# Layer 2's second token block: a step's seven w_ch1 products in one run, then its w_ch2 products in one run

## The chip, the cores and the metric

The kernel runs on one core of one Trainium2 chip. The metric is the device time of one execution in microseconds (us); lower is better. The median of three runs before the change is 657.65 us (657.61 to 657.93), so a difference of 0.2%, about 1.3 us, is near what a measurement of this kernel can tell from none.

## The reference

Three layers follow one another on 4 x 576 tokens of 512 features, all in float32: a retention (linear attention with decay), a gated layer that mixes along the sequence, and a plain feed-forward layer. The change lies in the third, which the kernel calls layer 2:

```python
def _moe2_ref(x, g_ln, w_ch1, w_ch2) -> np.ndarray:
    mu = np.mean(x, axis=-1, keepdims=True)
    var = np.mean((x - mu) ** 2, axis=-1, keepdims=True)
    xn = (x - mu) / np.sqrt(var + 1e-06) * g_ln
    ch = np.maximum(xn @ w_ch1, 0.0) @ w_ch2
    return (x + ch).astype(np.float32)
```

w_ch1 is 512 x 2048 and w_ch2 is 2048 x 512.

## The kernel before

**Three matmuls for one product.** Each float32 operand is split into a high part, rounded to the format that TensorE takes, and a low part, the rest. `mm3` (lines 134 to 137) forms high x high, high x low and low x high into one PSUM bank. So all products of the kernel come in threes.

**Layer 2.** Its 18 tiles of 128 tokens are worked in three blocks of six tiles. A block has eight steps (`NQ = 8`), so s runs from 0 to 23; a step makes 256 of the 2048 hidden features, as two halves of 128. Both dimensions of a step's first multiplication are halved and its eight block products are replaced by seven (Strassen's scheme in Winograd's form): features and weights are first added and subtracted (`mix_features`, `mix_w1`), then seven products are made, w0 to w6, of six matmuls of 384 columns each, and their results are added up by VectorE (DVE) into four quarters of hidden features. ScalarE (ACT) takes the relu of a quarter as its high part h (line 1175), and DVE subtracts it from the value for the low part (line 1176). `product` issues one of the seven, `hidden` a step's seven in four parts: w0 and w5, w1 and w2, w3 and w4, w6.

**The second multiplication** is `project(s, q)` for the four quarters q: three token tiles, each by `mm3` with 512 columns, nine matmuls, added over the eight steps of a block in six PSUM banks (`o_t`). Two banks are left for the seven products. In blocks 0 and 1 the parts of step s alternate with the four `project(s - 1, q)`. The third block (s of 16 and more, `hidden_kept`) only makes and keeps hidden features, seven products in one run; its second multiplication is done at the end by a seven-product scheme of its own (`multiply_kept`), whose weights `turning` prepares during blocks 1 and 2.

**Order.** Nothing is scheduled by a tool: each engine runs its instructions in the order in which the code emits them, and waits in place for semaphores. The loop `for s in range(NB * NQ)` is that order. Within a step, for q = 0 to 3, it emits a part of `hidden`, one `project`, one piece of `turning` (GpSimd, called POOL, and ACT), the split of w_ch2 rows into high and low (`split_w2`: ACT line 944, POOL line 945), their loading (`load_w2`) and saving for the third block (`save_w2`), then `ahead`, which loads rows, normalises them for the next block (DVE, ACT, POOL), writes the turned rows to DRAM (`norm`, line 994), loads them back as features and splits these (`mix_features`, `split_features`), and last `fetch_w1`, which brings the split w_ch1 of a later step back from DRAM. All transfers are issued by one queue, SP, in that order, and an SP instruction that waits holds back all behind it.

**Buffers.** w_ch1 has two (`w1_at`, steps even and odd), w_ch2 one for each half (`w2_at`), rows seven, taken in turn (`row_tile`).

Of the kernel before, what the change touches and what calls it, by code (L numbers as in the profile page):

```python
# [31 lines left out]
TB = 6  # L32
# [69 lines left out]
def kernel(  # L102
# [844 lines left out]
    def save_w2(s):  # L947
        if NF <= s < 2 * NK:
            p, i = divmod(s - NF, 2)
# [31 lines left out]

    def norm(p, n):
        z = yh[n]

        def stats():
# [4 lines left out]
            def rest():  # L990
                normed(z, st)
                yield
                t = row_tile()
                dve.transpose(out=t, in_=z)
                nc.sync.dma_start(out=z_dram[n], in_=t)
# [36 lines left out]
    def split_features(blk):  # L1032
        b11, b21, b12, b22 = halves(blk)
        for i, y in ((0, b11), (4, mixed(0)), (5, mixed(1)), (6, mixed(2)), (2, mixed(3)), (1, b21), (3, b22)):
# [138 lines left out]
    def relu(s, i, v):  # L1173
        t = h_t[s, i] = h_at[i][s % len(h_at[i])]
        act.activation(out=t[:, 0], in_=v, func=ACTF.Relu)  # L1175
        dve.scalar_tensor_tensor(  # L1176
# [3 lines left out]
    def hidden(s):  # L1180
# [5 lines left out]
        for part in ((0, 5), (1, 2), (3, 4), (6,)) if s else ((5, 0, 2, 4), (1,), (3,), (6,)):  # L1186
            for w in part:
# [9 lines left out]
                elif w == 2 or w == 4:  # L1197
                    dve.tensor_tensor(out=t, in0=v, in1=u if w == 2 else t, op=ALU.add)
                    if w == 4:
                        relu(s, 3, t)  # L1200
                else:
# [4 lines left out]
                    relu(s, {1: 0, 3: 2, 6: 1}[w], v)  # L1206
                if last:
                    free(bk[a])
            yield

# [48 lines left out]
    def project(s, q):  # L1259
# [4 lines left out]
        if p == 0 and q == 0:  # L1264
            o_t[blk] = [bank() for j in range(TB)]
        first, last = p == 0 and i == 0, p == NQ - 1 and i == 1
        w = w2_at[i]
        for j in reversed(range(TB // 2)):
# [3 lines left out]
            if last:  # L1272
                n = blk * TB + h * TB // 2 + j

                o = row_tile()
                dve.tensor_tensor(
                    out=turned_row(o), in0=ps.rearrange("p (f k c) -> p f k c", k=KE, c=32),
                    in1=o_s.pop(n).rearrange("p (f k c) -> p f k c", k=KE, c=32), op=ALU.add,
                )
                free(ps)  # L1280
                store_row(n, o)
# [112 lines left out]
    def ahead(blk, q):  # L1394
# [4 lines left out]
        if q == 1 and blk:  # L1399
            for j in reversed(range(TB // 2, TB)):  # L1400
                load_rest((blk - 1) * TB + j)
        if blk + 1 < NB:
# [6 lines left out]
            if q in (13, 20):  # L1409
                load_features(blk + 1, q // 20)  # L1410
            if q in (15 + blk, 22 + blk):
# [12 lines left out]
            if q >= 24 and q != 28:  # L1424
# [3 lines left out]
        if q == 4 * NQ - 1:  # L1428
            for j in reversed(range(TB // 2)) if blk + 1 < NB else range(TB):
                load_rest(blk * TB + j)  # L1430
            if blk + 1 == NB:
                o_s[None] = row_tile()
# [140 lines left out]
```

## Time and profile before

| | us |
|---|---|
| median of three runs | 657.65 |
| the profiled execution | 658.18 |
| its span, first to last instruction | 656.2 |
| around the span | 1.98 |
| TensorE (PE) busy, share of the span | 646.8, 99% |
| VectorE (DVE) busy | 455.0, 69% |
| GpSimd (POOL) busy | 321.6, 49% |
| ScalarE (ACT) busy | 316.0, 48% |

Two records stand for a matmul: PE is the multiplication, PEld the loading of its stationary operand. A busy PE is not a PE at its best: matmuls overlap, so each lasts longer in the records than the time to the next one's start. The distance from start to start is what a run of matmuls costs. In the trace, layer 2's first step begins at 282.0 us, block 1 (s = 8) at 399.26, the third block's first step without `project` (s = 17) at 540.73, and `multiply_kept` at 591.7.

### The profile page before, as it was taken

Reading aid. Unit: us, or ns where it says so; the run is one execution under the profiler, and the core shown is the slowest. Engines: PE = TensorE matmul, PEld = TensorE weight load, DVE = VectorE, ACT = ScalarE, POOL = GpSimd, SP = SyncE. Lnnn points to the kernel's source line nnn. Section 1 sums busy time; section 2 is a strip of 40 time slices with the busy share of each in tenths; the row PEclk is TensorE's granted clock in tenths of the full one; section 3 lists DMA queues with packets and bytes.
Section 4 is the critical chain, followed back from the end, with each engine's and each line's share of the span. In section 5 each row is a group of like instructions: output and inputs, shape, how many; then the busy total and the mean of one; then the engine's idle time right before and its main releaser. Section 6 shows DMA issues by size and latency. Waiting matters only on the chain.

```text
span 656.2 us, 12551 instructions
## 1 busy us (share of the span) xinstructions
PE 646.8 (99%) x4422; PEld 591.2 (90%) x4422; DVE 455.0 (69%) x906; ACT 316.0 (48%) x656; POOL 321.6 (49%) x315
## 2 busy tenths in 40 slices
PE   8998999999999999999999999999999999999997
PEld 5998899899889889899888999888988899999996
DVE  4698779789989885868888533555533345458894
ACT  4556795365286466434453533233535313335443
POOL 2467868225326528945655793265559743310000
PEclk9999999999999999999999999999999999999999
DMA  8999447777797695489896867799999699999634
GB/s 306 383 368 371 166 111 213 252 238 233 259 298 232 189 242 145 151 312 384 319 309 238 274 205 261 247 366 387 347 332 360 216 295 350 371 379 405 243 129 161
DMA packets 99264, 181.22 MB, mean 276 GB/s; under 512 B 9857, under 2 KB 46849, under 8 KB 97410
## 3 DMA queue, kind: packets, MB, share of 16 engines
q1 hardware_dynamic: 99202, 180.42, 81.5%
q8 instruction: 35, 0.57, 0.3%
q14 instruction: 27, 0.22, 0.1%
HBM read 122.97 MB, written 56.62 MB: 274 GB/s over the span
## 4 chain that ended last, share of the span: by engine, by line
PE 71%; DVE 3%; ACT 3%; DMA 1%; issue 1%; POOL 1%; SPq 0%; POOLq 0%; ACTq 0%; DVEq 0%
PE b L137 20%; PE b L136 20%; PE b L135 20%; PE b L864 4%; PE b L1341 3%; PE b L1342 2%; DVE c L163 1%; DMA raw<-in_w_ch_dram 1%; ACT t L695 1%; PE b L798 1%; POOL vnl L721 1%; PE b L797 0%; ACT t L692 0%; ACT raw L160 0%; DVE bs L669 0%
## 5 line engine op out<-in xcount | busy, mean ns | idle before, releaser
L137 PE MATMUL b<-fe,w 128*128 128x384 f32 x336 | 113.1, 337 | 0.0
L135 PE MATMUL b<-fe,w 128*128 128x384 f32 x336 | 112.9, 336 | 0.0
L136 PE MATMUL b<-fe,w 128*128 128x384 f32 x336 | 112.7, 335 | 0.0
L137 PE MATMUL b<-w,h 128*128 128x512 f32 (+1 forms) x270 | 98.1, 363 | 0.0
L136 PE MATMUL b<-w,h 128*128 128x512 f32 (+1 forms) x270 | 98.0, 363 | 0.0
L135 PE MATMUL b<-w,h 128*128 128x512 f32 (+1 forms) x270 | 96.8, 358 | 0.0
L945 POOL TENSOR_TENSOR w<-raw_w,w 128x512 fp32r<-128x512 f32 x30 | 39.6, 1320 | 59.0 <-ACT w L944 53.3
L135 PEld LDWEIGHTS b<-fe,w 128*128 128x128 f32 x336 | 63.1, 188 | 3.0
L136 PEld LDWEIGHTS b<-fe,w 128*128 128x128 f32 x336 | 63.1, 188 | 2.8
L137 PEld LDWEIGHTS b<-fe,w 128*128 128x128 f32 x336 | 63.0, 188 | 0.0
L137 PEld LDWEIGHTS b<-w,h 128*128 128x128 f32 x270 | 51.0, 189 | 7.6
L160 ACT ACTIVATE raw<-raw 128x512 f32<-128x512 f32 x44 | 29.9, 679 | 56.2 <-DVE b L158 49.3
L136 PEld LDWEIGHTS b<-w,h 128*128 128x128 f32 x270 | 50.9, 189 | 6.3 <-POOL w L945 0.2
L135 PEld LDWEIGHTS b<-w,h 128*128 128x128 f32 x270 | 51.0, 189 | 6.0 <-issue 0.2
L1175 ACT ACTIVATE h<-b 128x384 fp32r<-128x384 f32 x32 | 15.7, 492 | 83.8 <-DVE b L1204 54.1
L665 POOL TENSOR_TENSOR st<-st,par 128x1 f32<-128x1 f32 x36 | 22.1, 617 | 52.7 <-DVE st L664 52.2
L1176 DVE SCALAR_TENSOR_TENSOR h<-b,h 128x384 fp32r<-128x384 f32 x32 | 17.8, 556 | 30.9 <-ACT h L1175 30.9
L137 PE MATMUL b<-w_sg,vnl 128*128 128x288 f32 x128 | 37.8, 295 | 0.2 <-POOL vnl L721 0.2
L135 PE MATMUL b<-w_sg,vnh 128*128 128x288 f32 x128 | 37.8, 295 | 0.0
L137 PE MATMUL b<-xt_hi,w_in 128*128 128x288 f32 x128 | 37.7, 295 | 0.0
L136 PE MATMUL b<-w_sg,vnh 128*128 128x288 f32 x128 | 37.7, 295 | 0.0
L136 PE MATMUL b<-xt_lo,w_in 128*128 128x288 f32 x128 | 37.7, 294 | 0.0
(199 smaller groups left out, 1700.8 us busy)
## 6 DMA issues: line engine op xcount, KB each, us to landing
w<-ws_dram SPq DMA_DIRECT2D x96, 256.0 KB, 4.8
raw<-in_w_ch_dram SPq DMA_DIRECT2D x32, 512.0 KB, 5.0
ws_dram<-w SPq DMA_DIRECT2D x16, 896.0 KB, 7.4
w<-wb_dram SPq DMA_DIRECT2D x14, 1024.0 KB, 5.6
qv<-in_attn_dram SPq DMA_DIRECT2D x15, 576.0 KB, 6.8
w_dram<-c SPq DMA_DIRECT2D x32, 256.0 KB, 3.1
wb_dram<-fe SPq DMA_DIRECT2D x32, 256.0 KB, 5.1
kk<-in_attn_dram SPq DMA_DIRECT2D x15, 544.0 KB, 7.7
```

Source lines behind the costliest of these rows:

```text
L135: pe.matmul(ps, lh, rh, start=first, stop=False, skip_group_check=True)
L136: pe.matmul(ps, lh, rl, start=False, stop=False, skip_group_check=True)
L137: pe.matmul(ps, ll, rh, start=False, stop=last, skip_group_check=True)
L160: act.activation(out=f(w1), in_=f(w1), func=ACTF.Square)
L163: dve.scalar_tensor_tensor(out=f(c), in0=f(w1), scalar=F64_LEAST ** 2, in1=f(r), op0=ALU.is_ge, op1=ALU.mult)
L665: pool.tensor_tensor(out=st[:, 4:5], in0=st[:, 3:4], in1=col(par, O_MH), op=ALU.pow)
L864: pe.matmul(ps, g, wo[k][:, w], start=done[0] == 1, stop=done[0] == 3 * KE, skip_group_check=True)
L945: pool.tensor_tensor(out=t[:, 1], in0=raw, in1=f(t[:, 0]), op=ALU.subtract)
L1175: act.activation(out=t[:, 0], in_=v, func=ACTF.Relu)
L1176: dve.scalar_tensor_tensor(out=t[:, 1], in0=v, scalar=0.0, in1=f(t[:, 0]), op0=ALU.max, op1=ALU.subtract)
L1341: pe.matmul(ps, e[:, 0, x], t, start=begin, stop=False, skip_group_check=True)
L1342: pe.matmul(ps[:, 0:256], e[:, 1, x], t[:, 0:256], start=False, stop=end, skip_group_check=True)
```

## The change

It touches block 1 (s = 8 to 15), and the end of block 0.

- **Products.** `hidden_once` makes a step's seven products in one run of 42 matmuls, in the order w0, w5, w1, w2, w4, w3, w6, and then its own four `project(s, q)` follow in one run of 36, in the order of quarters 3, 2, 0, 1. At the end of block 0 the four `project(7, q)` stand behind one another. The two banks are handed over inside the run: w2 takes the one that w5 leaves, w4 the one that w1 leaves, for which DVE first copies w1's result with the relu to a new tile z. All low parts of h stand at the end of the step's DVE work.
- **Inside `project`** of block 1, but for the tiles that end a block, the three kinds of matmul are the outer loop and the three token tiles the inner one, so that consecutive matmuls write three banks in turn.
- **Transfers.** A step's `load_w2` and `fetch_w1` are issued right behind the first two products and behind the seventh; all else of the step comes later. Rows that `project` adds to at the end of a block are loaded at q = 28 and 29 of block 0 and q = 20 and 21 of block 1, where before it was at the block's last q and in the next block's second. Half of the `save_w2` moves from block 1 to the steps 4 to 7 of block 0. Turned rows for the third block are written to DRAM together.
- **Splits.** The low parts of the third block's features go from POOL to DVE and stand in steps 14 and 15 in another order. `turning` begins its pieces five q apart and puts them a step behind their loads.

```diff
@@ def save_w2(s):
-        if NF <= s < 2 * NK:
-            p, i = divmod(s - NF, 2)
+        if NQ <= s < NF + NQ:
+            p, i = divmod(s % NF, 2)
@@ def split_features(blk):
-            (pool if blk else dve).tensor_tensor(out=lo, in0=y, in1=f(hi), op=ALU.subtract)
+            (pool if blk == 1 else dve).tensor_tensor(out=lo, in0=y, in1=f(hi), op=ALU.subtract)
@@
+    def hidden_once(s):
+        u = t2.tile([128, TH], F32, tag="u", name="u")
+        t = t2.tile([128, TH], F32, tag="v", bufs=1, name="t")
+        z = t2.tile([128, TH], F32, tag="z", bufs=1, name="z")
+        bk = {}
+        for w in (0, 5, 1, 2, 4, 3, 6):
+            x, a, first, last = HIDDEN[w]
+            if first:
+                bk[a] = bank()
+            product(s, bk[a], w, x, first, last)
+            v = bk[a][:, 0:TH]
+            if w == 0:
+                act.copy(u, v)
+            elif w == 1:
+                dve.tensor_scalar(out=z, in0=v, scalar1=0.0, scalar2=None, op0=ALU.max)
+            elif w == 2 or w == 4:
+                dve.tensor_tensor(out=t, in0=v, in1=u if w == 2 else t, op=ALU.add)
+                if w == 2:
+                    relu(s, 0, z)
+                else:
+                    relu(s, 3, t)
+            elif w == 3:
+                dve.tensor_tensor(out=v, in0=v, in1=u, op=ALU.add)
+                relu(s, 2, v)
+                relu_low(s, 3, t)
+            else:
+                dve.tensor_tensor(out=u, in0=v, in1=u, op=ALU.add)
+                if w == 6:
+                    relu(s, 1, u)
+            if last and w != 3:
+                free(bk[a])
+            if w == 5:
+                yield
+        relu_low(s, 2, bk[2][:, 0:TH])
+        free(bk[2])
+        relu_low(s, 0, z)
+        relu_low(s, 1, u)
+        yield
@@ def project(s, q, begin=0):
+        js = list(reversed(range(TB // 2)))
+        for x, y in ((0, 0), (0, 1), (1, 0)) if begin and not last else ():
+            for j in js:
+                pe.matmul(
+                    o_t[blk][h * TB // 2 + j], t[:, x, j * 128:(j + 1) * 128], w[:, y], start=first and x == y,
+                    stop=False, skip_group_check=True,
+                )
@@ def turning():
-            start, pace = (3 + 4 * p, 1) if p < 5 else (8 * p - 8, 2)
-            for o in (0, 1, 1, 2, 2, 3, 4, 5):
+            start, pace = (3 + 5 * p - 3 * (p == 5), 1) if p < 6 else (8 * p - 8, 2)
+            for o in (0, 4, 4, 5, 5, 8, 8, 9) if p < 5 else (0, 8, 8, 9, 9, 12, 12, 13) if p < 6 else (0, 1, 1, 2, 2, 3, 4, 5):
@@ for s in range(NB * NQ):
-        steps = hidden(s) if s < NK else hidden_kept(s)
+        if s < NQ:
+            steps = hidden(s)
+        elif s < NK:
+            steps = hidden_once(s)
+            next(steps)
+            split_w2(2 * s + 1)
+            split_w2(2 * s)
+            load_w2(2 * s + 3)
+            load_w2(2 * s + 2)
+            fetch_w1(s + 1, 3)
+            next(steps)
+            for q in range(3):
+                fetch_w1(s + 2, q)
+        else:
+            steps = hidden_kept(s)
         for q in range(4):
-            next(steps)
-            if 0 < s <= NK:
+            if NQ <= s < NK:
+                project(s, (3, 2, 0, 1)[q], 1)
+            else:
+                next(steps)
+            if 0 < s < NQ:
                 project(s - 1, q)
...
+        if s == NQ - 1:
+            split_w2(2 * s + 1)
+            load_w2(2 * s + 3)
+            save_w2(2 * s + 1)
+            for q in range(4):
+                project(s, q)
```

TensorE (PE) in block 1, before: the end of a part of `hidden` in step 9 (fe are the features, w1 the weights) and the `project` of a quarter behind it (w2, h), up to the next part.

```order
L137 MATMUL b3_78<-fe_4319,w1_3372 128x384
L135 MATMUL b2_77<-w2_3373,h_3478 128x512
L136 MATMUL b2_77<-w2_3373,h_3478 128x512
L137 MATMUL b2_77<-w2_3373,h_3478 128x512
L135 MATMUL b7_82<-w2_3373,h_3478 128x512
L136 MATMUL b7_82<-w2_3373,h_3478 128x512
L137 MATMUL b7_82<-w2_3373,h_3478 128x512
L135 MATMUL b6_81<-w2_3373,h_3478 128x512
L136 MATMUL b6_81<-w2_3373,h_3478 128x512
L137 MATMUL b6_81<-w2_3373,h_3478 128x512
L135 MATMUL b4_79<-fe_4319,w1_3371 128x384
```

TensorE in block 1, now: the end of the run of 42 and the begin of the run of 36, of which four are shown.

```order
L135 MATMUL b6_81<-fe_4323,w1_3466 128x384
L136 MATMUL b6_81<-fe_4323,w1_3466 128x384
L137 MATMUL b6_81<-fe_4323,w1_3467 128x384
L1328 MATMUL b2_77<-w2_3373,h_3483 128x512
L1328 MATMUL b3_78<-w2_3373,h_3483 128x512
L1328 MATMUL b5_80<-w2_3373,h_3483 128x512
L1328 MATMUL b2_77<-w2_3373,h_3483 128x512
```

From the start of layer 2 to `multiply_kept`, a 512-column run followed a 384-column one 64 times and the other way round 64 times; now it is 36 and 36. No matmul is added or dropped.

VectorE (DVE) in block 1, now: one step's work on the seven products, from w5's sum to the last low part.

```order
L1255 TENSOR_TENSOR u<-b_79,u 128x384
L1243 TENSOR_SCALAR z<-b_81 128x384
L1245 TENSOR_TENSOR t<-b_79,u 128x384
L1245 TENSOR_TENSOR t<-b_81,t 128x384
L1251 TENSOR_TENSOR b_79<-b_79,u 128x384
L1190 SCALAR_TENSOR_TENSOR h<-t,h 128x384
L1255 TENSOR_TENSOR u<-b_81,u 128x384
L1190 SCALAR_TENSOR_TENSOR h<-b_79,h 128x384
L1190 SCALAR_TENSOR_TENSOR h<-z,h 128x384
L1190 SCALAR_TENSOR_TENSOR h<-u,h 128x384
```

Before, nine such instructions of a step stood among the normalisation of rows (statistics, transposes) piece by piece; now all ten stand together, and a step's other DVE work behind them.

GpSimd (POOL) from step 14 on, before: the split of w_ch2 rows (L945), and mixing (L1029) and low parts (L1037) of the third block's features.

```order
L945 TENSOR_TENSOR w_3373<-raw_w_5348,w_3373 128x512
L1029 TENSOR_TENSOR mix<-x 128x768
L1037 TENSOR_TENSOR fe<-x,fe 128x768
L1029 TENSOR_TENSOR mix<-x,mix 128x768
L1037 TENSOR_TENSOR fe<-mix,fe 128x768
L945 TENSOR_TENSOR w_3373<-raw_w_5411,w_3373 128x512
```

GpSimd from step 14 on, now: both splits of w_ch2 first, four mixings (L1038), then two pieces of `turning` (L967, L961), then step 15's splits.

```order
L945 TENSOR_TENSOR w_3373<-raw_w_5342,w_3373 128x512
L945 TENSOR_TENSOR w_3373<-raw_w_5344,w_3373 128x512
L1038 TENSOR_TENSOR mix<-x 128x768
L1038 TENSOR_TENSOR mix<-x,mix 128x768 x2
L1038 TENSOR_TENSOR mix<-x 128x768
L967 TENSOR_TENSOR fe<-raw_turn,fe 128x256 x4
L961 TENSOR_TENSOR raw_turn<-raw_turn 128x256 x2
L945 TENSOR_TENSOR w_3373<-raw_w_5483,w_3373 128x512
L945 TENSOR_TENSOR w_3373<-raw_w_5485,w_3373 128x512
```

The low parts of the features have left this engine, and step 15's splits of w_ch2 stand behind all of step 14's mixing and turning.

## Rows read from the trace of the kernel before

**Rows 1.** The page: busy us, share of the span and instructions of each engine.

```profile
PE 646.8 (99%) x4422; PEld 591.2 (90%) x4422; DVE 455.0 (69%) x906; ACT 316.0 (48%) x656; POOL 321.6 (49%) x315
```

**Rows 2.** Longest wait of PE, whole span; PEld's only one, 399 to 525.

```profile
PE b L519 <- ACT zero L515: 2.3, 1, 2.3
...
PEld b L136 <- POOL w L945: 0.2, 1, 0.2
```

**Rows 3.** Stretches: PE, PEld, DVE, ACT, POOL busy us (instructions), clock, DMA share, GB/s.

```profile
493.60:509.30 15.70, 15.70 (x79) 14.14 (x78) 5.13 (x10) 7.98 (x14) 14.16 (x11) 1.00 1.04 364
...
399.20:540.70 141.50, 141.50 (x703) 127.18 (x703) 64.87 (x138) 50.90 (x103) 80.86 (x80) 1.00 0.95 318
```

**Rows 4.** PE in order of time, layer 2: start, duration, engine, line, operation.

```profile
399.26 0.33 PE L135 MATMUL b<-fe,w 128*128 128x384 f32 x1
...
444.41 0.39 PE L135 MATMUL b<-w,h 128*128 128x512 f32 x1
...
446.49 0.33 PE L135 MATMUL b<-fe,w 128*128 128x384 f32 x1
...
540.73 0.33 PE L135 MATMUL b<-fe,w 128*128 128x384 f32 x1
...
548.04 0.33 PE L135 MATMUL b<-fe,w 128*128 128x384 f32 x1
...
555.32 0.33 PE L135 MATMUL b<-fe,w 128*128 128x384 f32 x1
```

**Rows 5.** PE in order of time, layer 1: 512 columns behind 288.

```profile
114.02 0.39 PE L135 MATMUL b<-w_in,xt_hi 128*128 128x512 f32 x1
...
115.18 0.39 PE L137 MATMUL b<-w_in,xt_lo 128*128 128x512 f32 x1
...
128.32 0.39 PE L135 MATMUL b<-w_in,xt_hi 128*128 128x512 f32 x1
...
135.12 0.39 PE L135 MATMUL b<-w_in,xt_hi 128*128 128x512 f32 x1
```

**Rows 6.** PE in order of time: two neighbours at the wait in layer 2.

```profile
425.69 0.50 PE L136 MATMUL b<-w,h 128*128 128x512 f32 x1
426.03 0.40 PE L137 MATMUL b<-w,h 128*128 128x512 f32 x1
```

**Rows 7.** A step of the third block: DVE and PE in order of time.

```profile
552.39 0.56 DVE L1231 TENSOR_TENSOR t<-b,u 128x384 f32<-128x384 f32 x1 [1.45 <-PE b L137]
...
552.20 0.33 PE L135 MATMUL b<-fe,w 128*128 128x384 f32 x1
...
553.24 0.33 PE L135 MATMUL b<-fe,w 128*128 128x384 f32 x1
```

**Rows 8.** Groups of DVE, 415 to 525: count, busy us, mean ns, idle before.

```profile
L1176 DVE SCALAR_TENSOR_TENSOR h<-u,h 128x384 fp32r<-128x384 f32 x8 | 7.2, 900 | 5.2 <-ACT h L1175 5.2
...
L1204 DVE TENSOR_TENSOR b<-b,u 128x384 f32<-128x384 f32 x7 | 4.0, 567 | 15.2 <-PE b L137 15.2
```

**Rows 9.** Groups of POOL, 415 to 525; DVE's feature splits: min, median, max ns.

```profile
L945 POOL TENSOR_TENSOR w<-raw_w,w 128x512 fp32r<-128x512 f32 x14 | 18.2, 1297 | 25.4 <-ACT w L944 19.7 <-DMA z_dram<-row 5.2 <-DMA w<-ws_dram 0.5
L967 POOL TENSOR_TENSOR fe<-raw_turn,fe 128x256 fp32r<-128x256 f32 x20 | 15.1, 789 | 0.0
L961 POOL TENSOR_TENSOR raw_turn<-raw_turn 128x256 f32<-128x256 f32 x20 | 14.8, 738 | 16.9 <-DMA raw_turn<-w_dram 15.6 <-DMA raw_w<-w_dram 0.6
...
L1029 POOL TENSOR_TENSOR mix<-x 128x768 f32<-128x768 f32 x2 | 3.7, 1845 | 0.1
...
L1037 DVE TENSOR_TENSOR fe<-x_raw,fe x5: 951/1925/2231, 255.3 to 279.0; 128x768 fp32r<-128x768 f32 x5
```

**Rows 10.** Transfers, 399 to 541: KB each, median us from issue to landing.

```profile
w<-ws_dram SPq DMA_DIRECT2D x54, 256.0 KB, 4.9
```

**Rows 11.** In order of time: a split of w_ch2 (POOL), storing a `turning` piece (SP).

```profile
401.67 1.30 POOL L945 TENSOR_TENSOR w<-raw_w,w 128x512 fp32r<-128x512 f32 x1
...
448.77 3.24 SPq L970 DMA_DIRECT2D wb_dram<-fe  x4
```

More of the change, by code (lines that the diff above doesn't have):

```diff
@@ L980, in load_y, with store_z @@
         nc.sync.dma_start(out=yh[n], in_=y_dram[n])
+    z_out = []
+    def store_z():
+        for n, t in z_out:
+            nc.sync.dma_start(out=z_dram[n], in_=t)
+        z_out.clear()
     def norm(p, n):
@@ L994, in rest @@
                 dve.transpose(out=t, in_=z)
-                nc.sync.dma_start(out=z_dram[n], in_=t)
+                z_out.append((n, t))
+                if p is t1 or n < 2 * TB:
+                    store_z()
             after(2, rest)
@@ L1263, in project @@
         t = h_t.pop((s, q))
-        if p == 0 and q == 0:
+        if blk not in o_t:
             o_t[blk] = [bank() for j in range(TB)]
-        first, last = p == 0 and i == 0, p == NQ - 1 and i == 1
+        first, last = p == 0 and i == begin, p == NQ - 1 and i != begin
         w = w2_at[i]
-        for j in reversed(range(TB // 2)):
+        js = list(reversed(range(TB // 2)))
[5 more added lines that the diff above has]
+                )
+        for j in () if begin and not last else js:
             c = slice(j * 128, (j + 1) * 128)
@@ L1271, in project @@
             mm3(ps, t[:, 0, c], t[:, 1, c], w[:, 0], w[:, 1], first, last)
[L1272 to L1281, printed above, removed]
+            if not last:
+                continue
+            n = blk * TB + h * TB // 2 + j
+            o = row_tile()
+            dve.tensor_tensor(
+                out=turned_row(o), in0=ps.rearrange("p (f k c) -> p f k c", k=KE, c=32),
+                in1=o_s.pop(n).rearrange("p (f k c) -> p f k c", k=KE, c=32), op=ALU.add,
+            )
+            free(ps)
+            store_row(n, o)
     def load_rest(n):
@@ L1398, in ahead @@
         n = (blk + 1) * TB
-        if q == 1 and blk:
-            for j in reversed(range(TB // 2, TB)):
-                load_rest((blk - 1) * TB + j)
+        x = q - (28, 20, 64)[blk]
+        if x in (0, 1):
+            for j in reversed(range(TB // 2)):
+                load_rest(blk * TB + x * TB // 2 + j)
         if blk + 1 < NB:
@@ L1423, in ahead @@
                 next(feat[0])
-            if q >= 24 and q != 28:
+            if blk:
+                if q == 24:
+                    next(feat[0])
+                for _ in range((1, 1, 1, 1, 2, 1)[q - 24] if 24 <= q < 30 else 0):
+                    next(feat[1])
+                if q in (25, 26):
+                    next(feat[0])
+            elif q >= 24 and q != 28:
                 if q > 24:
@@ L1427, in ahead @@
                 next(feat[1])
-        if q == 4 * NQ - 1:
-            for j in reversed(range(TB // 2)) if blk + 1 < NB else range(TB):
+        if q == 4 * NQ - 1 and blk + 1 == NB:
+            for j in range(TB):
                 load_rest(blk * TB + j)
-            if blk + 1 == NB:
-                o_s[None] = row_tile()
+            o_s[None] = row_tile()
     def keep():
@@ L1502 @@
             ahead(*divmod(4 * s + q, 4 * NQ))
+            if NQ <= s < NK:
+                next(turns, None)
             if q < 2 and s:
@@ L1506 @@
                 save_w1(s, q - 2 + s)
-            if q == 0:
-                fetch_w1(s + 1, 3)
-            else:
-                fetch_w1(s + 2, q - 1)
+            if not NQ <= s < NK:
+                if q == 0:
+                    fetch_w1(s + 1, 3)
+                else:
+                    fetch_w1(s + 2, q - 1)
+        store_z()
+        if s == NQ - 1:
+            split_w2(2 * s + 1)
+            load_w2(2 * s + 3)
+            save_w2(2 * s + 1)
+            for q in range(4):
+                project(s, q)
     for _ in multiply_kept(NB - 1):
```

40 lines of the change are left out of this document (25 added, 15 removed).

## Prediction

> **What bounds the kernel now.** I read the page first: TensorE is busy for 99% of the span and no other engine for more than 69% [rows 1]. Then the waits of TensorE: the longest of the whole run is 2.3 us at its start, and in the stretch that the change touches there is one, 0.2 us, of a weight load for POOL's split of w_ch2 [rows 2]; it moves one matmul's successor from 0.23 us behind it to 0.34 [rows 6], so it costs 0.10. The table by stretch says who comes next: in step 14 DMA's share is 1.04 and POOL is busy for 14.16 of the 15.7 us, while TensorE's granted clock stays at 1.00, the 2.4 GHz level [rows 3]. A change that adds and drops no matmul can then gain only in the distance from one matmul's start to the next, and lose where TensorE begins to wait.
>
> So I read those distances. Undisturbed, in the third block, a step's 42 matmuls of 384 columns take from 548.04 to 555.32, 7.28 us or 173.3 ns each. The same 42 directly behind 512-column ones take from 540.73 to 548.04, 7.31 [rows 4]: the change of kind costs 0.03, and resolved to single matmuls it is the first six that stand wider. Nine 512-column matmuls between two parts of `hidden` take from 444.41 to 446.49, 2.08 us [rows 4]. What 512 columns cost undisturbed is seen in layer 1: 30 from 128.32 to 135.12, 226.7 ns each [rows 5], so nine would be 2.04 and this change of kind costs 0.04. Does a longer run come to rest? In layer 1 a 512-column run begins behind 288 columns; its first five matmuls take 1.16 us (114.02 to 115.18) instead of 1.13, and from there on the distance is 226.7 [rows 5]. A run that never has more than nine members doesn't show where it ends behind 384 columns; I take nine.
>
> **The change: what it saves.** Per step of block 1 the changes of kind fall from four pairs to one; with the joined runs at the end of block 0 they fall from 64 pairs to 36 in all. I make the sum over the stretch from the start of step 8 to that of step 17, now 540.73 - 399.26 = 141.47 us [rows 4]. In the changed kernel the same work is: `project(7)`, which goes on with a 512-column run, 36 x 0.2267 = 8.16; eight times a run of 42, 7.31, and a run of 36, 8.16 + 0.04 = 8.20; and step 16's 42, 7.31. That is 8.16 + 8 x 15.51 + 7.31 = 139.55, or 1.92 less, 0.10 of it the wait that I take to go, since both splits of w_ch2 now stand in front of a whole run of 42. The bounds: if a run of 36 never came to rest, it would cost 4 x 2.08 = 8.32, the sum 140.67 and the gain 0.80. If joining cost nothing at all at a run's start, the gain would be 1.92 + 8 x 0.04 = 2.24. I take the middle, since the rows of layer 1 do come to rest.
>
> Beside this stands a rule. The Trainium skill, "TensorE: Matmul & The Clock Gate", section "Back-to-back issue gap", gives the warm distance as the columns divided by 2.4 GHz plus 2.5 ns, whatever stood before. By that it is an estimate of 215.8 ns for 512 columns and 162.5 for 384, and order would be worth nothing, so that the sum would be the 0.10 alone. This case's rows disagree: 226.7 and 173.3 undisturbed, and more behind a change of kind.
>
> **What it may add.** (1) Banks. The seven products now have two banks in one run. With the run's start as zero, products end at 1.07, 2.11 (w5), 3.15 (w1), 4.19 (w2), 5.23 (w4), 6.27 (w3) and 7.31 (w6). w2 writes the bank that DVE's sum of w5 reads: it starts about 0.2 us after 2.11 and lasts 0.56, as in the third block, where the sum behind w2 starts 0.19 us after w2's last slot (552.20 to 552.39), ends at 552.95, and the product that needs its bank starts at 553.24 without a gap [rows 7]. That leaves 0.2 to 0.3 us. w4 waits in the same way for z; no row shows z's instruction, and I bound it by none below 0.5 and by 0.57, a sum that reads PSUM with 384 columns [rows 8]: it spares 0.25 too. So I cost it at nothing, as long as DVE is free when w5 ends.
>
> (2) DVE's remainder. Its sums follow the products, the first low part follows w3's; from w6's sum, which ends at 8.2, three more low parts run, 0.56 from PSUM and two of up to 0.90 from SBUF [rows 8]: 10.6. All else that it does in the step must be through by the next run's w5, 15.5 + 2.3 = 17.8: 7.2 us of room. What it does besides is 64.87 - 9 x 9 x 0.6 = 16 us in the whole stretch [rows 3], nearly all in four steps, 4 us each. The worst is step 14, four feature splits of 0.95 to 2.23 [rows 9]: 3.8 to 8.9, near 5 as POOL waits for half of them. It fits but for the upper end, which is 1.4 late, once. The first low part, needed at 7.31 + 0.68 + 0.68 = 8.7, is there at 7.7.
>
> (3) POOL in steps 14 and 15. The splits end at about 5.1. Two mixings run to 8.8; the third writes a buffer whose low part DVE makes only behind its ten, at about 12.9, and the fourth likewise. Then come four low parts of 0.79 and two subtractions of 0.74, and only behind them step 15's split: 12.9 + 2 x 1.85 + 3.16 + 1.48 + 1.30 = 22.5 [rows 9], or 7.0 in step 15's own count. `project(15, 3)` needs it at 7.31 + 0.69 = 8.0. It spares 1 us; with mixings slowed by DVE it could be 0.5 to 1 late.
>
> (4) SP behind step 15. Six stores of rows wait for the last sums, then one piece of `turning` takes 3.24 us to issue [rows 11], and only then is step 17's last w_ch1 fetched, about 7 us into step 16; with 4.9 us to land [rows 10] it is there at 12, needed at 7.31 + 6.27 = 13.6. Step 18's first two products are fetched behind it, there at 13, needed at 14.6. Both spare 1.5 us; in the other steps the fetches are now earlier than before.
>
> (5) `project(7, 2)` needs the split of w_ch2 that POOL ends in the kernel before at 401.67 + 1.30 = 402.97 [rows 11]; it starts at 399.26 + 4.1 = 403.4 plus 0.2 to the low part. The saves of w_ch2 that move to steps 4 to 7 leave block 1, where DMA has the least room. I cost both at nothing.
>
> The sum is 658.18 - 1.92 = 656.26 for a profiled execution, of which the median of the runs was 0.53 below: 657.65 - 1.92 = 655.7 us, 0.29% faster.
>
> **The rivals.** *A feeder late once or twice*: (3) or (4), or DVE at the upper end of (2), takes back 0.5 to 1.4 us: 656.2 to 657.1. For it speaks how little each spares, against it that each needs several rows at their upper ends. Chance 0.16, half of it short of the 0.2% that can be told.
>
> *The long run never rests*: each 512-column matmul stays at 231 ns, gain 0.80, 656.85. For it: no run behind 384 columns is seen past nine, and consecutive matmuls now change banks each time. Against it: rows 5. Chance 0.10.
>
> *Order is worth nothing*: the 0.27 us that a mixed step takes above its parts is in the kinds of products and not in their change, so only the wait is saved: 657.55. Against it: a mixed step of (141.47 - 0.10) / 9 = 15.71 less four times 2.08 leaves 7.39 for its 42, which alone take 7.28 [rows 4]. Chance 0.03. It is what the quoted section would make of the change.
>
> *Two banks are too few*: w2 and w4 wait for DVE in each of the eight steps. It ends slower by over 0.2% once a step loses more than (1.92 + 1.32) / 8 = 0.41 us, that is, when DVE begins w5's sum some 0.65 us later than its 0.2 behind the product in each step (the 0.25 spared and the loss), or the handover from DVE to TensorE takes that much. For it: the 0.2 us spared is less than one of DVE's instructions, any of which may stand in front. Against it: rows 7, the same distance without a gap, and 7.2 us of room. At 0.5 us a step: 657.65 - 1.92 + 4 = 659.7. Chance 0.13, of it 0.08 slower and 0.05 within 0.2%.
>
> **How the numbers follow.** The forecast, all covers holding, has 0.58: 655.7, by itself 655.3 to 656.2. Faster by over 0.2%: 0.58 + 0.08 = 0.66. Within: 0.08 + 0.10 + 0.03 + 0.05 = 0.26. Slower: 0.08. The range from 655.3 (just past the bound of 2.24) to 657.3 takes in the late feeder and the run that doesn't rest, and leaves out the two last rivals, 0.16, or most of it.
>
> **What would show it.** In the changed profile a step of block 1 should take 15.51 us from first product to first product, its 42 matmuls 7.31 and its 36 8.20, with distances of 226.7 ns from the tenth on. TensorE should have no wait for DVE at the first matmul of w2 and of w4, none for POOL at `project(15, 3)`, and none for a transfer in steps 17 and 18. I am wrong if distances of 231 ns go on to the end of a run, or if a gap of some tenths stands at w2 in every step.

## The result: 0.8% slower

The changed kernel takes 662.92 us (median of six runs, 661.81 to 664.67) against 657.67 before: 1.0082 times as long, 95% interval 1.0069 to 1.0095. The forecast, 655.7, had a gain of 0.3%.

The profile after: first the page's busy line, which answers to [rows 1], then the waits of PE in block 1, which answer to [rows 2] (who waits for whom; us in total, times, the longest).

```profile
PE 648.7 (98%) x4422; PEld 591.5 (89%) x4422; DVE 465.0 (70%) x921; ACT 316.2 (48%) x656; POOL 311.1 (47%) x308
```

```profile
PE b L135 <- ACT u L1241: 3.0, 2, 2.7
PE b L135 <- DVE u L1255: 1.2, 1, 1.2
```

DVE (10.0 us) and PE (1.9) are busy for longer than before, the other engines for at most 0.3 us longer, and yet TensorE waits, 2.7 us at the longest. Where, the order of its matmuls shows (start, duration, what they are):

```profile
408.69 0.33 PE L135 MATMUL b<-fe,w 128*128 128x384 f32 x1
...
416.00 0.63 PE L1328 MATMUL b<-w,h 128*128 128x512 f32 x2
...
424.20 0.33 PE L135 MATMUL b<-fe,w 128*128 128x384 f32 x1
...
473.74 0.34 PE L137 MATMUL b<-fe,w 128*128 128x384 f32 x1
475.32 0.45 PE L135 MATMUL b<-fe,w 128*128 128x384 f32 x1 [1.24 <-DVE u L1255]
...
490.38 0.34 PE L137 MATMUL b<-fe,w 128*128 128x384 f32 x1
491.01 0.45 PE L135 MATMUL b<-fe,w 128*128 128x384 f32 x1 [0.29 <-ACT u L1241]
...
506.48 0.34 PE L137 MATMUL b<-fe,w 128*128 128x384 f32 x1
509.49 0.67 PE L135 MATMUL b<-fe,w 128*128 128x384 f32 x1 [2.68 <-ACT u L1241]
```

Step 8 takes 15.51 us (408.69 to 424.20), the 42 matmuls of its products 7.31: the forecast's figures. So do steps 9 and 11, and step 10 takes 15.54. But w2's first matmul comes 1.58 us behind its neighbour in step 12 (473.74 to 475.32, the 19th of the run), and another 0.6 us is lost at the start of that step's run of 36, which waits for its relus. In steps 13 and 14 it is w1's first, the 13th of the run, that comes 0.63 us (490.38 to 491.01) and 3.01 us (506.48 to 509.49) behind its neighbour. Steps 12, 13 and 14 take 17.68, 16.10 and 20.03, together 7.3 above 15.51. This profile also loses 1.3 us in block 0, in steps 4 and 5, a loss that comes and goes (below). The two losses less the 1.9 us of the forecast's gain make 6.7; the profiled execution took 6.5 longer (664.67 against 658.18).

The same by stretches (busy us and instructions of PE, PEld, DVE, ACT and POOL, granted clock, DMA share, GB/s): steps 8, 12 and 14, then the gap in step 14 and what follows it.

```profile
408.69:424.20 15.51, 15.51 (x80) 14.06 (x78) 6.52 (x12) 3.59 (x7) 2.55 (x2) 1.00 0.82 271
470.77:488.44 17.67, 16.34 (x79) 13.91 (x78) 9.36 (x22) 7.52 (x16) 6.23 (x8) 1.00 0.94 293
504.55:524.58 20.03, 17.35 (x80) 15.59 (x78) 9.71 (x14) 9.76 (x19) 10.15 (x6) 0.91 1.05 368
506.50:509.50 3.00, 0.32 (x3) 0.01 (x1) 0.03 (x1) 2.55 (x6) 0.00 (x0) 1.00 1.08 365
509.50:513.00 3.50, 3.50 (x11) 3.50 (x12) 1.09 (x2) 1.50 (x3) 2.96 (x3) 0.51 1.05 387
```

Behind the gap the granted clock is 0.51, the 1.2 GHz level, for 3.5 us: the 384-column matmuls stand 0.320 us apart instead of 0.173, which adds some 1.6 us. So step 14's 4.5 us are 2.9 of waiting and 1.6 of clock.

**Where the waits begin.** w2 takes the bank that w5 leaves, so in step 12 it waits for DVE's sum of w5 (L1255). w1 is added to w0 in w0's bank, so in steps 13 and 14 it waits for ACT's copy of w0 (L1241). Both engines had little to do: in the gap of step 14 ACT does the scaling and the copy behind it, DVE nothing. Each has an instruction at its head that waits for a transfer. DVE, in steps 11 to 13 (in brackets the idle time before, and what ended it):

```profile
473.64 0.69 DVE L669 BATCH_NORM_STATS2 bs<-row 128x6 f32<-128x512 f32 x1 [4.10 <-DMA row<-y_dram]
...
474.71 0.55 DVE L1255 TENSOR_TENSOR u<-b,u 128x384 f32<-128x384 f32 x1
...
486.69 0.69 DVE L669 BATCH_NORM_STATS2 bs<-row 128x6 f32<-128x512 f32 x1 [2.69 <-DMA row<-y_dram]
```

L1255 is w5's sum; it could have run at 473.1 and stood behind the statistics of a row that had not landed. The last row, at 486.69, is late too. ACT, steps 11 to 14:

```profile
459.45 1.24 ACT L944 CAST w<-raw_w 128x512 fp32r<-128x512 f32 x2 [2.46 <-DMA z_dram<-row]
...
477.81 1.18 ACT L944 CAST w<-raw_w 128x512 fp32r<-128x512 f32 x2 [5.30 <-DMA wb_dram<-w]
...
489.78 0.82 ACT L692 ACTIVATE row<-row,st 128x512 f32<-128x512 f32 x1 [2.84 <-DVE st L689]
490.50 0.46 ACT L1241 COPY u<-b 128x384 f32<-128x384 f32 x1
...
506.95 2.13 ACT L1024 ACTIVATE x<-x,par 128x384 f32<-128x384 f32 x4 [8.01 <-DMA x<-z_dram]
508.98 0.46 ACT L1241 COPY u<-b 128x384 f32<-128x384 f32 x1
```

L1241 is the copy of w0. In step 13 it stands behind L692, which normalises the last row and waits for its statistics; in step 14 behind L1024, the scaling of the third block's features, which waits 8.01 us for their transfer. And SP, which issues all transfers (start, time to issue, what, how many):

```profile
434.40 1.74 SPq L951 DMA_DIRECT2D wb_dram<-w  x3
...
444.68 1.57 SPq L939 DMA_DIRECT2D raw_w<-w_dram  x2
446.34 3.97 SPq L931 DMA_DIRECT2D w<-ws_dram  x8
450.37 1.89 SPq L957 DMA_DIRECT2D raw_turn<-w_dram  x2
452.31 2.75 SPq L951 DMA_DIRECT2D wb_dram<-w  x3
...
461.48 1.57 SPq L939 DMA_DIRECT2D raw_w<-w_dram  x2
463.14 3.78 SPq L931 DMA_DIRECT2D w<-ws_dram  x8
466.97 0.47 SPq L980 DMA_DIRECT2D row<-y_dram  x1
```

The row of 473.64 was issued at 466.97, behind step 11's loading (L939) and eight fetches (L931); these waited for the splits of w_ch2; these, at 459.45, for the save (L951) of step 10, which reads the buffer that they write and was itself issued behind step 10's fetches, at 452.31 (the bracket names the store of a row, issued behind that save). It is a loop: split, load, fetch, save, landing, next split. The load starts 3.7 us into steps 8 and 9, then 5.0, 6.2 and 12.2 us into steps 10, 11 and 12.

From step 11 on the casts wait for saves. Step 10's 1.3 us have another source, on POOL:

```profile
441.33 0.55 POOL L665 TENSOR_TENSOR st<-st,par 128x1 f32<-128x1 f32 x1 [5.97 <-DVE st L664]
441.85 1.56 POOL L961 TENSOR_TENSOR raw_turn<-raw_turn 128x256 f32<-128x256 f32 x2
443.36 2.54 POOL L945 TENSOR_TENSOR w<-raw_w,w 128x512 fp32r<-128x512 f32 x2
```

The split (L945) stands behind two subtractions of `turning`, and these behind the numbers of a row that was issued at 433.83, behind step 9's fetches. `turning`'s next load (L957) then stands in front of step 10's save. So late rows and `turning` give the loop its first push. In run 4 below, which has no saves to wait for, step 10's load is nearly as late (4.7 us) and step 11's is back at 3.7.

### The profile page after: what moved, and what is told of

The parts are those of the page before. It is cut to its first block, busy times and chain, and to the rows that moved or that the text cites. A ratio compares the mean times of both kernels' runs of the same rounds, so it can differ in the third digit from the quotient of the medians.

```text
span 662.9 us, 12587 instructions
## 1 busy us (share of the span) xinstructions
PE 648.7 (98%) x4422; PEld 591.5 (89%) x4422; DVE 465.0 (70%) x921; ACT 316.2 (48%) x656; POOL 311.1 (47%) x308
## 4 chain that ended last, share of the span: by engine, by line
PE 70%; DMA 11%; DVE 7%; ACT 5%; issue 3%; POOL 2%; SPq 1%; ACTq 0%; POOLq 0%; DVEq 0%
PE b L135 15%; PE b L137 15%; PE b L136 15%; PE b L1328 6%; PE b L864 6%; PE b L1406 3%; DMA kk<-in_attn_dram 2%; DMA z_dram<-row 2%; PE b L327 2%; PE b L256 2%; DMA raw_w<-w_dram 2%; DMA w<-ws_dram 2%; PE b L1407 2%; PE b L318 1%; DMA ws_dram<-w 1%
## 5 line engine op out<-in xcount | busy, mean ns | idle before, releaser
L945 POOL TENSOR_TENSOR w<-raw_w,w 128x512 fp32r<-128x512 f32 x30 | 39.1, 1315 | 56.7 <-ACT w L944 33.2
L1328 PE MATMUL b<-w,h 128*128 128x512 f32 x270 | 63.2, 391 | 0.1
L137 PE MATMUL b<-w,h 128*128 128x512 f32 (+1 forms) x180 | 62.3, 346 | 0.0
L136 PE MATMUL b<-w,h 128*128 128x512 f32 (+1 forms) x180 | 62.3, 346 | 0.0
L135 PE MATMUL b<-w,h 128*128 128x512 f32 (+1 forms) x180 | 61.8, 343 | 0.0
L1328 PEld LDWEIGHTS b<-w,h 128*128 128x128 f32 x270 | 50.4, 188 | 11.0 <-ACT h L1186 0.4
L137 PE MATMUL b<-xt_hi,w_in 128*128 128x288 f32 x128 | 37.7, 295 | 0.0
L137 PEld LDWEIGHTS b<-w,h 128*128 128x128 f32 x180 | 34.1, 189 | 4.1
L135 PE MATMUL b<-xt_hi,w_in 128*128 128x288 f32 x128 | 37.7, 294 | 0.0
L135 PEld LDWEIGHTS b<-w,h 128*128 128x128 f32 x180 | 34.1, 189 | 3.5 <-issue 0.2
```

Of the source, the lines that this page charges most:

```text
L135: pe.matmul(ps, lh, rh, start=first, stop=False, skip_group_check=True)
L136: pe.matmul(ps, lh, rl, start=False, stop=False, skip_group_check=True)
L137: pe.matmul(ps, ll, rh, start=False, stop=last, skip_group_check=True)
L945: pool.tensor_tensor(out=t[:, 1], in0=raw, in1=f(t[:, 0]), op=ALU.subtract)
L1328: pe.matmul(o_t[blk][h * TB // 2 + j], t[:, x, j * 128:(j + 1) * 128], w[:, y], start=first and x == y, stop=False, skip_group_check=True,)
```

## The experiments

Each kernel is the changed one with the edit shown. The table has the length of steps, from first product to first product, in each profile (three steps for 17 to 19), and the time against the kernel before. The first row's times are those above; the others were compared on the same chip as the kernel before, whose runs were wider spread there (655.6 to 660.6 in all).

| kernel | 12 | 13 | 14 | 16 | 17-19 | median | ratio, interval |
|---|---|---|---|---|---|---|---|
| changed | 17.68 | 16.10 | 20.03 | 7.31 | 21.84 | 662.92 | 1.0082, 1.0069-1.0095 |
| 1 saves first | 15.51 | 16.21 | 20.71 | 7.31 | 21.84 | 659.9 | 1.0042, 1.0028-1.0056 |
| 2 rows early | 17.07 | 15.54 | 20.63 | 7.31 | 21.84 | 660.9 | 1.0050, 1.0032-1.0069 |
| 3 scaling later | 16.21 | 16.47 | 15.51 | 7.33 | 21.84 | 658.33 | 1.0011, 0.9999-1.0024 |
| 4 saves in block 0 | 15.54 | 15.54 | 19.43 | 7.31 | 21.84 | 659.85 | 1.0041, 1.0016-1.0066 |
| 5 three cures | 15.54 | 15.51 | 16.24 | 7.73 | 21.84 | 656.44 | 0.9987, 0.9969-1.0006 |
| 6 norm early | 16.45 | 15.51 | 15.86 | 7.30 | 21.84 | 657.87 | 1.0009, 0.9988-1.0030 |
| 7 fetches spread | 15.51 | 15.51 | 15.54 | 7.69 | 23.99 | 658.1 | 1.0017, 1.0002-1.0033 |
| 8 cures, saves in block 1 | 15.54 | 15.54 | 17.67 | 7.87 | 21.99 | 660.31 | 1.0045, 1.0025-1.0066 |
| 9 spread to step 13 | 15.51 | 15.51 | 16.03 | 7.34 | 21.84 | 655.8 | 0.9973, 0.9962-0.9984 |
| 10 the same, inner order | 15.53 | 15.53 | 15.57 | 7.31 | 21.84 | 656.72 | 0.9994, 0.9983-1.0005 |
| 11 spread to step 11 | 15.54 | 15.54 | 18.91 | 7.31 | 21.84 | 660.41 | 1.0048, 1.0018-1.0079 |
| 12 changed again | 17.42 | 16.06 | 18.57 | 7.31 | 21.84 | 662.06 | 1.0068, 1.0048-1.0088 |

**1. Saves first.**

```diff
             split_w2(2 * s)
+            save_w2(2 * s + 1)
+            save_w2(2 * s)
             load_w2(2 * s + 3)
...
-            elif q == 1:
-                save_w2(2 * s + 1)
-                save_w2(2 * s)
```

> In block 1 a step's saves of w_ch2 are issued right behind its splits, ahead of the loading and the fetches, where the changed kernel issues them behind the fetches. Theory A (the root is the loop of split, load, fetch, save, and the next split into the same buffer, which is longer than a step, so that each step begins its transfers later than the one before): the lateness never builds up, steps 8 to 15 take 15.5 us each, the stalls of steps 12, 13 and 14 (7.3 us in the profile) go, and the time is 655.7 to 657.2, the upper end if block 0's 1.3 us stay. Theory B (rows and features are loaded too near to their use): no row moves, so steps 12 to 14 still lose 6 to 8 us and the time is 661.5 to 664. Theory C (two banks are too few): the same 661.5 to 664.

Half of theory A: step 12 is whole, and ACT's casts in it follow its copy at once (ACT and SP of this kernel; the first row is the save of step 11, 3.7 us into the step, where it stood 15.3 into it, at 470.58):

```profile
456.67 1.62 SPq L951 DMA_DIRECT2D wb_dram<-w  x3
```

```profile
469.82 0.48 ACT L1241 COPY u<-b 128x384 f32<-128x384 f32 x1 [3.50 <-PE b L137]
470.20 1.14 ACT L944 CAST w<-raw_w 128x512 fp32r<-128x512 f32 x2
```

But step 13 loses 0.7 us and step 14 5.2, no less than in the changed kernel. The loop alone is not their cause.

**2. Rows early.**

```diff
-                if q == at - (j > 0 and blk):
+                if q == at - (0, 1, 1, 1, 2, 3)[j] * blk:
```

> The last rows that block 1 normalises are loaded one or two q earlier (the fifth at q = 11, the sixth at q = 12), so that they no longer stand behind a step's fetches and DVE's statistics find them there; the saves stay where the changed kernel has them. Theory B (rows too near to their use): steps 12 and 13 take 15.5 us, and the features come early enough that step 14 loses little: 656 to 658.5. Theory A (the loop of the saves): DVE's 1.6 us at w2 of step 12 go, but ACT still waits some 5 us for the save of step 11 before the relus of step 12, and the later transfers are as late as before, so that 0.6 us in step 12 and 3 to 5 in step 14 stay: 659.5 to 662.

Most of theory A again: w2 of step 12 and the whole of step 13 lose nothing, so the late rows were the direct cause of their stalls, but the first matmul of step 12's run of 36, waiting for its relus, comes 1.43 us behind its neighbour, and step 14 loses 5.1 us.

**3. Scaling later.**

```diff
-            if q in (15 + 2 * blk, 22 + blk):
+            if q in (15 + 2 * blk, 22 + 42 * blk):
...
             fetch_w1(s + 1, 3)
+            if s == NK - 2:
+                scale_features(2, 1)
             next(steps)
```

> ACT's second scaling of the third block's features moves from the end of step 13 to step 14, behind ACT's copy of w0 and its casts of w_ch2, so that the wait for their transfer no longer stands in front of that copy. Nothing else changes. Both theories on the root (A, the loop of the saves; B, rows too near to their use) say that the last link of the chain alone is cut: the 3.0 us gap in step 14 goes, and with it the 1.5 us at the lower granted clock that follow, 662.9 - 4.5 = 658.4 (657.9 to 659.2). If the lower clock is not a consequence of the gap, 1.5 us stay: 659.9. If the mixing on GpSimd then comes too late for step 15, 1 to 2 us come back there.

As expected: step 14 takes 15.51, and 658.33 is the median. The clock falls no more, as it would if its fall follows the gap. Step 12, which lies in front of the edit, loses 0.7 us here and not 2.2: the row of 473.64 lands 1.4 us into the step in this profile, 2.8 in that of the changed kernel. So the size of a stall differs from one execution to the next.

**4. Saves in block 0.**

```diff
-        if NQ <= s < NF + NQ:
+        if 2 <= s < NF + 2:
```

> The saves of w_ch2 for the third block are all made in block 0 (steps 1 to 7) but for one pair in step 8; block 1 has none from step 9 on, and its order is otherwise that of the changed kernel. Theory A (the loop of the saves): no split in steps 9 to 15 waits for a save, steps 9 to 15 take 15.5 us: 655.7 to 657.5. Theory B (rows too near to their use): steps 12 to 14 still lose most of their 7.3 us, 661 to 664. A further theory, D (saves put into block 0 hold up its features, which the 1.3 us of steps 4 and 5 in the changed kernel's profile may be): steps 2 to 5 lose 1 to 3 us here.

Steps 9 to 13 are whole: with no saves between the fetches and the rows the stalls of steps 12 and 13 go. Step 13, which run 1 left, goes too, as its last row lands 3.0 us in front of the step here, 1.6 in run 1 and 1.8 in the changed kernel. Step 14 loses 4 us with no save near it, so it has a root of its own. Steps 3 to 5 lose 3.3 us against 15.7, more than theory D had said, in this one profile, that of the slowest of ten runs (665.28).

**5. Three cures.** Edits 1 to 3 together.

> The changed kernel with three edits together: the saves of w_ch2 right behind the splits (as in the first run), the last rows loaded one or two q earlier (as in the second), and the second scaling of features behind step 14's copy of w0 and its casts (as in the third). The runs so far say that the saves' loop makes the stalls of steps 12 and 13 and the place of the scaling that of step 14, each by itself. Then no step of block 1 loses more than 0.1 us, TensorE's granted clock stays at its upper level, and what the joined runs save shows alone: about 1.9 us below the kernel before, 655.7 (655.0 to 656.4, with up to 1.3 us of block 0 in the upper part). If the products' order had a cost that the stalls hid (theory C, two banks), the steps would be longer than 15.54 us and the time at or above that of the kernel before.

656.44: between the forecast and no change, its interval takes in 1. Steps 8 to 13 are whole. In step 14 the scaling now stands before the relus, and the first `project` comes 0.82 us behind its neighbour; in step 16 w3 comes 0.49 us behind its neighbour, as DVE is still at block 1's last row sums when w5 ends: a late feeder of nearly the size in the forecast's rivals, though not one that they name.

**6. Norm early.** Edit 1, and load and normalisation of the last two rows earlier.

```diff
+                if q == at - (0, 1, 1, 1, 2, 3)[j] * blk:
...
+                if q == at + 1 + (1, 0, 0, 0, -1, -2)[j] * blk:
```

> Saves right behind the splits, and of the last two rows of block 1 both the load (q = 11 and 12) and the normalisation (q = 13 and 14) come one or two q earlier, so that the sixth row's statistics stand in step 11 and not behind the ten DVE instructions of step 12's products; the scaling stays at the end of step 13. Theory E (the stall of step 14 is the chain of the sixth row: its statistics behind a step's DVE work, then ACT, transpose, store, load, scaling): the row is turned some 8 us earlier, the load of the features no longer waits in step 13, and step 14 takes 15.5 us: 655.0 to 657, as with the scaling moved. If the features' transfer itself is late for another reason (DMA's share), step 14 keeps 2 us or more: 658 to 660. If the row lands too late for its earlier statistics, DVE holds up w5's sum of step 12 by 1 to 2 us.

Both things happen: step 14 keeps 0.35 us of its 4.5. The features' load is issued 9.2 us into step 13, against 11.0 in the changed kernel and 10.6 in run 5, which has the early rows but not the early normalisation: so the chain of the sixth row does set when it is issued, as theory E says. That is 1.8 of the 3.2 us by which the scaling starts sooner; the rest is a quicker landing (run 7), which theory E does not explain. And DVE again stands before a row in transit, so that w2 of steps 10 and 12 comes 0.57 and 0.98 us behind its neighbour.

**7. Fetches spread.**

```diff
-            fetch_w1(s + 1, 3)
             next(steps)
-            for q in range(3):
-                fetch_w1(s + 2, q)
...
-            if not NQ <= s < NK:
-                if q == 0:
-                    fetch_w1(s + 1, 3)
-                else:
-                    fetch_w1(s + 2, q - 1)
+            if q == 0:
+                fetch_w1(s + 1, 3)
+            else:
+                fetch_w1(s + 2, q - 1)
```

> The changed kernel, but the fetches of w_ch1 go back among a step's four q, as before the change, behind the step's other transfers; loading and saves of w_ch2 stay where the changed kernel has them. Theory A (loop of split, load, fetch, save): six of the eight fetches no longer stand in the loop, it becomes some 3 us shorter than a step, and steps 9 to 13 take 15.5 us; step 14 keeps its 4 to 5.3 us: 659.5 to 661.5. If fetches first are needed for the products, TensorE waits for w_ch1 at a step's first product or at w6, 0.5 us or more in several steps, and the time is above 662.

Neither branch had foreseen this: all eight steps are whole, step 14 too, with saves, rows and scaling where the change has them. The rows of steps 13 and 14 say why (SP, then ACT, of this kernel, and of run 4 behind it):

```profile
492.81 1.85 SPq L1016 DMA_DIRECT2D x<-z_dram  x4
494.76 0.89 SPq L931 DMA_DIRECT2D w<-ws_dram  x2
...
498.93 2.14 ACT L1024 ACTIVATE x<-x,par 128x384 f32<-128x384 f32 x4 [4.90 <-DMA x<-z_dram]
```

```profile
499.38 1.86 SPq L1016 DMA_DIRECT2D x<-z_dram  x4
501.33 0.89 SPq L939 DMA_DIRECT2D raw_w<-w_dram  x2
502.27 6.40 SPq L931 DMA_DIRECT2D w<-ws_dram  x8
...
507.56 2.13 ACT L1024 ACTIVATE x<-x,par 128x384 f32<-128x384 f32 x4 [7.40 <-DMA x<-z_dram]
```

Two things are sooner. The features' load is issued 8.7 us into step 13 (492.81, the step at 484.12), against 11.0 in the changed kernel and 10.7 in run 11, where the stores of turned rows that it waits for stand behind step 12's eight fetches. And the scaling starts on it 4.3 us after its last issue (492.81 + 1.85 = 494.66 to 498.93), against 5.7 in the changed kernel and 6.3 in run 4, where the issue is but 0.5 us later in the step. ACT's copy in step 14 can bear a scaling that starts up to some 14.9 us behind step 13's first product, since one at 15.3 (run 6) costs 0.35 us and one at 15.45 (run 9) 0.5: here it starts at 14.8, in run 4 at 17.3, in the changed kernel at 18.5. What makes the landing longer is not settled: it is 4.1 to 4.3 us in runs 7, 9 and 10, with the fetches spread, and 5.7 to 6.3 in the changed kernel and runs 1, 2, 4, 11 and 12, with eight of them right behind the load, but 4.2 in run 6 with eight behind, and 6.1 in the kernel before. What the fetches in front were for shows in the third block: steps 17 to 19 take 2.15 us longer, and 0.8 of it is in the list of waits (PE, 399 to 560):

```profile
PE b L137 <- DMA w<-ws_dram: 0.6, 1, 0.6
PE b L135 <- DMA w<-ws_dram: 0.2, 1, 0.2
```

**8. Cures, saves in block 1.** Edits 1 to 3, and `save_w2` with its condition of before.

> The three cures together, and all saves of w_ch2 in block 1 (steps 8 to 15), as before the change; block 0 then has the transfers that it had before. Theory D (saves in block 0 hold up its features): steps 4 and 5 take 15.7 us in the profile, and the time is 0.3 to 1.3 us below that of the three cures alone. Theory A with saves in time: the four more pairs in steps 12 to 15 cost nothing, since each is issued right behind its splits: 654.8 to 656. Against it: block 1 has then DMA's share of before, 1.04 in step 14, and a late fetch in steps 15 to 17 could take back 0.5 to 2 us.

By the time it goes against both: block 0 is whole, as theory D had it, but step 14's casts wait 3.40 us for the raw w_ch2, whose load is issued 15.2 us into step 13 (12.5 in run 5), behind more transfers on the same queue, and the step loses 2.2 us. Beside the cures, at least, moving saves out of block 1 was worth while (656.44 in run 5).

**9. Spread to step 13.** Edit 7 for `s < NK - 2` alone, so that steps 14 and 15 keep their fetches in front.

> The changed kernel, with the fetches of w_ch1 put back among a step's four q in steps 8 to 13 and first, as the change has them, in steps 14 and 15 alone. Theory F (fetches in front hold up everything else on SP's queue: the saves on which the next splits wait, and the rows and turned rows of the next block's features; behind them the third block's first steps lack w_ch1): steps 8 to 15 stay at 15.5 us as in the run with all fetches spread, and the waits of steps 17 to 19 (2.2 us there) go: 655.3 to 656.5. If the third block's waits come from DMA's share and not from the order of issue, 1 us or more of them stays: 657 to 658.2.

Theory F holds: steps 17 to 19 are whole again, and the kernel is faster than the one before: 655.8, 0.9973 of it (0.9962 to 0.9984). Step 14 keeps 0.5 us, since the features land a little late (ACT of this kernel):

```profile
500.09 2.13 ACT L1024 ACTIVATE x<-x,par 128x384 f32<-128x384 f32 x4 [5.55 <-DMA x<-z_dram]
502.13 0.46 ACT L1241 COPY u<-b 128x384 f32<-128x384 f32 x1
```

**10. The same, inner order.** And `project` in block 1 by `mm3` for each tile.

> The same kernel, and project in block 1 makes the three matmuls of one token tile one behind the other, as before the change, instead of the three tiles in turn. If consecutive matmuls into three banks in turn matter for the distance (against the forecast, which gave that nothing), the 36 of a step take 8.3 us or more instead of 8.20, and the time is 0.8 us or more above; if they don't, the time and the steps are the same within 0.1 us a step.

A step takes 15.53 and its 512-column matmuls 227.6 ns, against 227.8: banks in turn matter nothing to the distance. Yet the median is 0.9 us higher, where the expectation had 0.8 or more if they mattered. No step of its profile is longer by more than 0.03 us, and it has fewer stalls than run 9's; the spreads overlap (654.6 to 658.4, 654.5 to 656.3), but its median lies above all of run 9's. This difference stays unexplained, and how much of run 9's gain would come again is open with it.

**11. Spread to step 11.** Edit 7 for steps 8 to 11.

> Fetches among the four q in steps 8 to 11 only, first in steps 12 to 15. It tells one root from two. Theory A with one root (lateness that builds up over steps 9 to 12 in the loop of the saves, whose last saves are made in step 11): all stalls of steps 12 to 14 are gone, 655.3 to 656.5. Theory F (two: the saves' loop for steps 12 and 13, and for step 14 the sixth row and the turned rows that stand behind the fetches of steps 12 and 13): steps 12 and 13 lose at most 0.7 us, step 14 still loses 3.5 to 5.3: 658.5 to 661.

Theory F: two roots. Steps 12 and 13 are whole, step 14 loses 3.4 us, without a fall of the clock.

**12. The changed kernel again.**

> The changed kernel once more, beside the others on their chip. Of its losses, those of steps 12 to 14 should come back at the same matmuls (w2 of step 12, the run of 36 of step 12, w2 of steps 13 and 14; 5 to 7.5 us together), since they follow from the order on the queues. Step 4's and 5's 1.3 us come back only if the saves put into block 0 cause them in each execution (theory D); five of the eight profiles of kernels with those same saves show at most 0.4 us there.

The stalls of steps 12 to 14 come back at the same matmuls as in the first profile, which in steps 13 and 14 are w1's and not w2's, as the expectation calls them; steps 4 and 5 lose nothing this time.

## Why the prediction was wrong

**The gain was as worked out.** The whole steps take 15.51 to 15.54 us, a 512-column run comes to rest (226.7 ns from the tenth matmul on and 227.8 on average, against 231.2 in block 0), and each change of kind costs what rows 4 and 5 had shown. In run 10 the forecast's stretch is 405.69 to 537.28 and 8.16 for `project(7)`, 139.75 us, where 139.55 was forecast. That rules out the run that never rests and order worth nothing. The Trainium skill's rule ("TensorE: Matmul & The Clock Gate", section "Back-to-back issue gap") on the warm distance, which the section gives for a matmul by itself, does not fit this trace: 227.8 and 173.3 ns, not 215.8 and 162.5, and with an order that counts.

**(1) and (2), where it broke.** (1) took the handover of the banks as free "as long as DVE is free when w5 ends". For w2 and w4 that held: in whole steps they show no wait, and two banks are enough. But (1) has no line for w1, which adds to w0's bank and needs ACT's copy of it. Before the change the nine matmuls of a `project`, 2.08 us, stood between w5 and w1; now w1 is due 2.1 us into the step. The trace of before could have shown it: in step 14, which begins at 493.61, this copy stands behind the same scaling and ends 2.6 us into the step.

```profile
495.76 0.46 ACT L1194 COPY u<-b 128x384 f32<-128x384 f32 x1
```

By this row the new order alone would have held w1 up by some 0.5 us there (an estimate); features that come later made it 2.9. And (2) asked whether DVE has time for its row work, by its busy time, and not whether that work's input has landed. In step 12 DVE had time and stood idle for 4.10 us before one row. ACT's queue, where the 3 us of step 14 arise, had no term at all.

**(4), the root.** SP was costed behind step 15 alone, with "in the other steps the fetches are now earlier than before" as pure gain. On one queue that means that saves, rows and features are later. Fetches in front of the saves close the loop that stalls step 12 (runs 1, 4 and 11); behind fetches and saves the last row comes too late for step 13 (runs 2, 4 and 11); fetches in front of the turned rows' stores, and perhaps those behind the features' load, stall step 14 (runs 7 and 11). The term missing was 7.3 us in the profile, 5.65 in that of run 12 without the fall of the clock, step 15's 0.13 included, against a gain of 1.9. The forecast's 0.08 for a slower kernel stood on a wait for DVE in each of the eight steps; the loss came in three of them, from inputs that had not landed.

**(3), (5) and the rest of (4)** held: no wait at `project(15, 3)`, none in steps 17 and 18; run 7 shows that fetches in front are worth 2.15 us there. A late feeder shows in step 16 of runs 5, 7 and 8, at 0.4 to 0.6 us, and not in runs 3, 6, 9 and 10, whose step 14 is whole or nearly so too; what decides is not shown. What (5) says of the saves moved to block 0 stays open: steps 2 to 5 lose from nothing (runs 2, 6, 7, 10, 12) to over 3 us (run 4) in single profiles; the two profiles without moved saves show none.

## What to carry to other kernels

When a change puts some transfers first on a queue, cost what now comes behind them, through to the engine whose next instruction waits for it: an in-order engine loses time to the input that its head waits for, however little it is busy. Look for loops in which a transfer out of a buffer must land before the buffer's next filling, add up one turn of it, and compare it with the step. Here, fetches first in the two steps whose data are urgent, and spread in the others, gave back in run 9 nearly what the order of products saves (655.8 against 657.35, and 656.7 in run 10). And where a new order brings two products closer together, look in the old trace at when the instruction between them ran.

## What was not expected of the hardware

**The granted clock after a gap.** A gap in TensorE's work was followed by ten or eleven matmuls at the 1.2 GHz level (0.320 us for 384 columns, which agrees with the cold distance that the section cited above gives, columns divided by 1.2 GHz), some 1.6 us lost, in four of the six profiles in which w1 of step 14 comes over 2 us late: after gaps of 2.41 (run 4) and 3.01 us (the changed kernel) at once, after 3.63 (run 2) and 3.69 us (run 1) some 0.5 and 0.9 us of work later. After 3.10 us (run 12) and 3.44 us (run 11) the clock stayed up, at distances of 0.17 to 0.19 from the second on. The same code, in run 12 and the first profile, shows both. PE of run 12 and the stretch behind its gap (columns as above):

```profile
504.29 0.34 PE L137 MATMUL b<-fe,w 128*128 128x384 f32 x1
507.40 0.44 PE L135 MATMUL b<-fe,w 128*128 128x384 f32 x1 [2.77 <-ACT u L1241]
```

```profile
507.40:510.50 3.10, 3.10 (x18) 3.10 (x19) 1.65 (x3) 1.51 (x3) 2.56 (x3) 1.00 1.06 389
```

So the length of the gap alone does not decide it; what else does was not tried.
